# Attention, Fourier mixing and feed-forward on one core: radix-4 sums of four tiles as matrix products, and every tile's sums turned by TensorE

## The chip, the cores and the metric

The kernel runs on one core of a Trainium2 chip. The metric is the device time of one execution in microseconds (us). A core has a matrix engine (TensorE, PE in the rows, with its weight loads as PEld), a vector engine (VectorE, DVE), a scalar engine (ScalarE, ACT), GpSimd (POOL), and a queue engine (SyncE, SP), which here issues all DMA transfers but the gathers. Each engine works through its own list of instructions strictly in order; an instruction that waits holds everything behind it on its engine.

## What is computed

Inputs are q, k, v of shape 8 x 8 x 576 x 64 (batch, heads, positions, width of a head) and two weight matrices of 512 x 2048 and 2048 x 512, stored in double precision. The output has 8 x 576 rows of 512.

```
scores = scale * np.matmul(q, k.transpose(0, 1, 3, 2))
mask = (rel >= 0) & (rel < window)            # window = 64
attn = softmax(where(mask, scores, -1e9)); x = attn @ v   # heads side by side: 512 columns
mixed = np.real(fft(fft(x, axis=1), axis=2))
u = x + mixed
un = (u - mu) / np.sqrt(var + 1e-06)
ch = np.maximum(un @ w_ch1, 0.0) @ w_ch2
return u + ch
```

## The kernel before

**Tiles.** The 4608 rows are cut into 36 tiles of 128 rows (T = 0 to 35), nine tiles for each pair of batches. `attn_tile(T)` does the attention of a tile: keys and queries are transposed (pk, pq), scores of two half tiles are formed (psc), masked and reduced by DVE (L587), put through exp on ACT (L595), transposed (pp, pt), and multiplied with the values into two banks pa, one for each half of the heads (L657). DVE divides each by the row sums (rc, L665 to L669) into xu. Tiles 0 to 12 work in single precision and are transposed by TensorE ("whole"). From tile 13 on operands are split in two half-precision parts, high and low, laid side by side in SBUF, and transposed by DMA transposes that SP issues (kst L487, qbd L499, pt L626).

**The radix-4 results.** The Fourier transform along the 512 columns starts with sums and differences of the four column quarters of xu: `radix4` writes them to y (L691, four instructions on DVE, or on POOL). They must be turned so that columns lie on partitions. Where `soon` is true (tiles 0 to 12, and tiles 4 and 8 of each nine, by `Y_SOON`) TensorE transposes y into a PSUM bank py, one of the four banks that also hold scores and pa (L750), and ACT copies it into yT. Otherwise (17 tiles, from 14 to 34) y is split: ACT writes the high part yp (L754), DVE the low part (L758), SP issues one DMA transpose of both (L765), and POOL or DVE adds the turned parts into yT (L718). yp shares a ring of one buffer, "up", with the split normalised rows up (L1032, L1035).

**Then** `fft(b)` folds yT, does the two transform stages on TensorE (pg L878, pz L910), and SP stores the result md to memory (L938), for the first batch also straight to the rows' tile mt (L955). `norm_tile(T)` gathers mt, adds it to xu, normalises (L1005 to L1016), splits (u_hi, u_lo L1035) and turns the rows (L1040). `ffn(c)` takes two tiles at a time: 18 chunks of 16 steps, ph (L1197), relu and its low part hh by ACT and DVE (L1212, L1215), po (L1178). Chunk 0 works in single precision. The weights are 32 pieces of 512 KB, converted by three DVE instructions each (L1089 to L1101) and squared by ACT (L1107).

**What sets the order.** Steps are recorded with `op(engine, duration, priority, ...)`, some with a second engine (`alt`), and `Plan.order()` simulates the core with these durations and latencies and writes every engine's list from that. So a changed constant can move instructions everywhere. Where the plan foresees a longer gap of TensorE ahead of the first ph, it puts matmuls on the identity there that compute nothing (warm, L1276).

Of the kernel before, what the change touches and what calls it, by code (L numbers as in the profile page):

```python
# [12 lines left out]
F32 = mybir.dt.float32  # L13
# [6 lines left out]
ALU = mybir.AluOpType  # L20
# [21 lines left out]
Y_SOON = (4, 8)  # L42
LAZY, LAZY_FFT, LAZY_U = 0.4, 0.4, 0.5
# [5 lines left out]
SLACK = 0.5  # L49
PLAIN = 1  # L50
W_DMA, W_DMA_STEP, W_CONV, W_SQ, W_SPLIT, W_STEP = -40, 1.0, 20, 60, 60, 0.3
# [74 lines left out]
class Op:  # L126
    __slots__ = ("eng", "dur", "lat", "fn", "deps", "outs", "prio", "wait", "ready", "allocs", "bufs", "idx", "durs", "margin", "port", "slack")


class Plan:  # L130
# [13 lines left out]
    def __init__(self, rings, fifo):  # L144
        self.rings, self.fifo, self.ops, self.gaps = dict(rings), fifo, [], []
        self.slack = 0.0

    def op(self, eng, dur, prio, fn, reads=(), writes=(), lat=0.0, alt=(), holds=(), port=True):
# [5 lines left out]
        o.port, o.slack = port, self.slack  # L154
# [41 lines left out]
    def order(self):  # L196
# [23 lines left out]
        while len(res) < n:  # L220
# [77 lines left out]
def attn_fft_ffn_kernel(ctx: ExitStack, tc: tile.TileContext, q, k, v, w1, w2, gidx, dft_d, dft_s, mask, out):  # L298
# [24 lines left out]
    ident = cp.tile([P, P], F32, name="ident")  # L323
    mhalf = cp.tile([P, 1], F32, name="mhalf")
# [37 lines left out]
    op("POOL", 0.3, -500, lambda: make_identity(nc, ident), writes=[Bid])  # L362
    op("POOL", 0.1, -499, lambda: nc.gpsimd.memset(mhalf, -0.5), writes=[Bmh])
# [47 lines left out]
    def attn_tile(T, base):  # L411
# [18 lines left out]
        op("DMA", 1.45, base - 8, lambda: load("kn", "kq", k), writes=[bk], lat=2.0)  # L430
        op("DMA", 1.45, base - 8, lambda: load("qn", "kq", q), writes=[bq], lat=2.0)
        if whole:
            op("DMA", 1.45, base - 6, lambda: load("vw", None, v), writes=[Bva[i]], lat=2.0)
        else:
            op("DMA", 1.45, base - 6, lambda: load("vn", None, v), writes=[bv], lat=2.0)
# [39 lines left out]
        else:  # L475
# [27 lines left out]
            op("DMA", TURN, base + 0.2, k_turn, [bkp], [bkT], lat=2.0)  # L503
            op("ACT", 0.95, base + 0.5, lambda e: q_part(0, e), [bq], Bfl[4:6], alt=("DVE", 0.6, lazy))
            op("POOL", 2.1, base + 0.6, lambda e: q_part(1, e), [bq], Bfl[4:6], alt=("DVE", 1.13, lazy))
            for j in range(2):
                op("DMA", TURN, base + 0.7, lambda j=j: q_turn(j), Bfl[4:6], [Bq[i]], lat=2.8)
        if T == PRO and n > 0:
# [14 lines left out]
            op("DVE", 1.6, base + 0.3, k_tail, [BkT[(T - 1) % 3]], [BkT[before], Buf("tail")])  # L523
# [33 lines left out]
        for jj in range(2):  # L557
# [74 lines left out]
            op("DMA", HTURN, base + 4.2 + jj, lambda g=p_turn: g(0), [bpp], [bt, bt2], lat=1.8)  # L632
            op("DMA", HTURN, base + 4.3 + jj, lambda g=p_turn: g(1), [bpp], [bt2], lat=1.8)
# [5 lines left out]
        for hf in range(2):  # L639
# [668 lines left out]
```

## Time and profile before

| | |
|---|---|
| median of the runs | 1010.4 us |
| runs | 1010.17, 1010.4, 1551.11 us |
| the profiled execution's own time | 1014.19 us |
| its span, first to last instruction | 1012.4 us |
| mean granted TensorE clock | 0.990 of full speed |
| instructions | 22555 |

Read it so: the span is what the trace covers; 1.8 us of the profiled time lie outside it. Busy shares tell how full an engine is, not whether it is waited for. A busy TensorE is not TensorE at its peak, since its matmuls are pipelined and overlap in the records; what counts is the distance from one group's start to the next one's. A granted clock below 1.00 in a stretch means that part of it ran at 1.2 instead of 2.4 GHz. Many single-precision matmuls stand as two records each, so an x8 of psc is four matmuls.

### The profile page before, as it was taken

The numbers are of one execution on the slowest core, as the hardware profiler recorded it, in microseconds if no ns is written. First come the engines' busy times: TensorE is split into PE (matmuls) and PEld (weight loads), VectorE is DVE, ScalarE is ACT, GpSimd is POOL, SyncE is SP. The second block draws the span as 40 slices with busy tenths as digits, with TensorE's granted clock in tenths as the row PEclk, the third lists the DMA queues.
The fourth block names the chain that finished last, engine by engine and source line by source line (L and its number), as shares of the span: only waits on it lengthen the run. The fifth ranks groups of instructions, "written<-read, shape, count | busy, mean of one in ns | idle before, by whom it ended". The sixth has DMA issues, their size and how long they took to land.

```text
span 1012.4 us, 22555 instructions
## 1 busy us (share of the span) xinstructions
PE 975.3 (96%) x8793; PEld 692.1 (68%) x8793; DVE 671.6 (66%) x1972; ACT 417.3 (41%) x1044; POOL 205.8 (20%) x211
## 2 busy tenths in 40 slices
PE   8888999999998999999999999999999999999998
PEld 6776768766675666666676667666676667666664
DVE  5889898887876758676776668666786555441121
ACT  6665667563544444344452345322454223211111
POOL 1001001133224403352132203141121300310000
PEclk9988999999999999999999999999999999999999
DMA  8978766533859896988768575857564411220000
GB/s 192 232 199 232 188 193 146 103 72 75 148 124 167 168 152 137 163 151 148 152 127 169 101 137 106 160 117 149 90 128 103 83 32 45 63 63 21 1 21 22
DMA packets 310955, 123.60 MB, mean 122 GB/s; under 512 B 292728, under 2 KB 292856, under 8 KB 310848
## 3 DMA queue, kind: packets, MB, share of 16 engines
q1 hardware_dynamic: 308128, 113.24, 55.3%
q0 software_dynamic: 2720, 8.92, 3.2%
q8 instruction: 69, 1.13, 0.5%
q14 instruction: 38, 0.31, 0.1%
HBM read 54.97 MB, written 14.17 MB: 68 GB/s over the span
## 4 chain that ended last, share of the span: by engine, by line
PE 73%; DMA 10%; DVE 9%; SPq 3%; ACT 2%; issue 2%; POOL 1%; DVEq 0%; ACTq 0%; POOLq 0%
PE ph L1197 31%; PE po L1178 28%; PE pa L657 3%; PE pg L878 2%; PE pz L910 2%; PE psc L568 2%; DMA uhl<-up 2%; DMA pt<-flex 2%; PE psc L575 2%; DMA kn<-in_k 1%; DMA mt<-md,gix 1%; DVE hh L1215 1%; SPq L626 1%; DMA qn<-in_q 1%; DVE y L691 1%
## 5 line engine op out<-in xcount | busy, mean ns | idle before, releaser
L1197 PE MATMUL ph<-uhl,w0s 128*128 128x256 f16 (+1 forms) x3384 | 427.5, 277 | 9.3 <-DVE hh L1215 8.6
L1178 PE MATMUL po<-w1s,hh 128*128 128x512 f16 (+1 forms) x1696 | 426.0, 387 | 0.2
L1197 PEld LDWEIGHTS <-w0s 128*128 128x128 f16 x3264 | 318.5, 98 | 96.8 <-issue 14.3
L1215 DVE SCALAR_TENSOR_TENSOR hh<-ph,hh 128x256 f16<-128x256 f32 x272 | 114.6, 422 | 223.8 <-ACT hh L1212 212.2
L1212 ACT ACTIVATE hh<-ph 128x256 f16<-128x256 f32 x272 | 104.1, 383 | 375.5 <-PE ph L1197 264.5
L1178 PEld LDWEIGHTS <-hh 128*128 128x128 f16 x1632 | 155.9, 98 | 139.5 <-issue 1.0
L595 ACT ACTIVATE pr<-pr,nm 128x128 f32<-128x128 f32 x288 | 91.3, 393 | 16.3 <-DVE nm L587 16.3
L587 DVE CUSTOM_DVE_ANT_0 pr<-psc,mskb 128x128 f32<-128x128 f32 x288 | 65.7, 286 | 15.9 <-PE psc L568 11.8
L1012 POOL TENSOR_TENSOR rs<-mv,mhalf 128x1 f32<-128x1 f32 x36 | 21.6, 599 | 181.0 <-DVE mv L1008 160.2
L1035 POOL TENSOR_TENSOR up<-un,up 128x512 f16<-128x512 f32 x33 | 39.0, 1183 | 70.4 <-ACT up L403 63.6
L620 POOL TENSOR_TENSOR flex<-pr,flex 128x512 f16<-128x512 f32 x25 | 30.0, 1202 | 109.5 <-ACT flex L403 90.7
L657 PE MATMUL pa<-va,pt 128*64 128x65 f16 (+1 forms) x760 | 41.5, 207 | 5.7 <-DMA pt<-flex 5.1
L988 POOL DMA_INDIRECT mt<-md,gix x34 | 35.9, 1057 | 52.0 <-DMA md<-mp 46.4
L657 PE MATMUL pa<-ve,pt 128*64 128x65 f16 (+1 forms) x760 | 42.0, 208 | 0.1
L484 POOL TENSOR_TENSOR flex<-kn,flex 128x512 f16<-128x512 f32 x19 | 22.7, 1197 | 83.6 <-ACT flex L403 82.1
L403 ACT CAST flex<-pr 128x512 f16<-128x512 f32 x38 | 23.5, 620 | 27.7 <-DMA pt<-flex 25.5
L669 DVE TENSOR_TENSOR xu<-pa,rc 128x256 f32<-128x256 f32 x72 | 30.6, 425 | 2.9 <-DMA out<-xu 0.3
L568 PE MATMUL psc<-kst,qbd 128*128 128x128 f32 x208 | 29.8, 293 | 2.5 <-ACT qbd L403 1.2
L691 DVE TENSOR_TENSOR y<-xu 128x256 f32<-128x256 f32 x70 | 30.2, 472 | 0.6
L657 PEld LDWEIGHTS <-pt 128*64 128x64 f16 x1104 | 20.8, 112 | 14.0 <-issue 7.2
L568 PEld LDWEIGHTS psc<-kst,qbd 128*128 128x128 f32 x208 | 26.9, 203 | 4.5 <-issue 1.9
L910 PE MATMUL pz<-g,ds__75 97*96 97x257 f16 (+3 forms) x240 | 29.2, 273 | 0.5 <-DVE g L888 0.5
(156 smaller groups left out, 1115.1 us busy)
## 6 DMA issues: line engine op xcount, KB each, us to landing
wd<-in_moe_w_ch SPq DMA_DIRECT2D x20, 512.0 KB
out<-xu SPq DMA_DIRECT2D x36, 256.0 KB
ve<-va SPq DMA_DIRECT2D x67, 130.0 KB
kn<-in_k SPq DMA_DIRECT2D x32, 256.0 KB
qn<-in_q SPq DMA_DIRECT2D x32, 256.0 KB
flex<-in_moe_w_ch SPq DMA_DIRECT2D x12, 512.0 KB
flex<-in_v SPq DMA_DIRECT2D x20, 256.0 KB
md<-mp SPq DMA_DIRECT2D x24, 192.0 KB
```

Of the source, the lines that this page charges most:

```text
L568: nc.tensor.matmul(p_[:, hp], qw, keys(hp, jj), start=True, stop=True)
L587: nc.vector.tensor_tensor_reduce(out=t["pr", jj][:, hp], in0=t["ps", jj][:, hp], in1=mskb[:, m : m + P], scale=-0.125, scalar=3.0e38, op0= ...
L595: nc.scalar.activation(pr, pr, AF.Exp, bias=t["nm", jj][:, hp : hp + 1], scale=-1.0)
L657: nc.tensor.matmul(pa[64 * jj : 64 * jj + 64, hh], pt[:, sl], v_, start=(x == 0), stop=(x == len(mm) - 1))
L691: eng.tensor_tensor(out=o, in0=p0, in1=p1, op=al)
L910: nc.tensor.matmul(pz[:M, c0:c1], ds_[:NJ, a, c[0] : c[0] + c[1]], t["g", gi][:, b_, c0:c1], start=(x == 0), stop=(x == len(mm) - 1),)
L988: nc.gpsimd.indirect_dma_start(out=mts[T], out_offset=None, in_=mds[pb][0 : HR if n < 4 else 2 * HR], in_offset=bass.IndirectOffsetOnAxis( ...
L1035: eng.tensor_tensor(out=t["up"][:, 1], in0=t["un"], in1=t["up"][:, 0], op=ALU.subtract)
L1178: nc.tensor.matmul(t["po"][i], l_, r_, start=(f == 0 and x == 0), stop=(f == NKF - 1 and x == len(mm) - 1))
L1197: nc.tensor.matmul(ph, l_, r_, start=(x == 0), stop=(x == len(mm) - 1))
L1212: nc.scalar.activation(t["hh", f][:, 0], ph, AF.Relu)
L1215: nc.vector.scalar_tensor_tensor(out=hh[:, 1], in0=ph, scalar=0.0, in1=hh[:, 0], op0=ALU.max, op1=ALU.subtract)
```

## The change

Every tile now has `soon` true, so the two-part way (yp, its DMA transpose, the addition) is run no more. For tiles 1 to 4 `radix4` is not recorded at all: TensorE forms the sums itself while it turns the tile, as products of a quarter of xu with the identity or with its negative, added up in PSUM, 12 products in place of 4 transposes. The division by the row sums is cut in two, the reciprocal on DVE and the multiplication on DVE or ACT; on ACT it is four instructions of 64 columns, one for each head. Constants of the plan change: estimated DMA latencies rise, priorities of the weights' conversion fall, and a new margin makes steps on other engines start later behind their producers.

```diff
-Y_SOON = (4, 8)
-LAZY, LAZY_FFT, LAZY_U = 0.4, 0.4, 0.5
+Y_SOON = (0, 1, 2, 3, 4, 5, 6, 7, 8)
+LAZY, LAZY_FFT, LAZY_U = 0.4, 0.8, 0.2
-SLACK = 0.5
+SLACK = 1.0
+SLACK_V = 0.3
+WARY = 0
+LAZY_N = -0.8
+Y_SUMS = (1, 2, 3, 4)
-W_DMA, W_DMA_STEP, W_CONV, W_SQ, W_SPLIT, W_STEP = -40, 1.0, 20, 60, 60, 0.3
+W_DMA, W_DMA_STEP, W_CONV, W_SQ, W_SPLIT, W_STEP = -40, 1.0, 40, 70, 50, 0.3
...
+    op("POOL", 0.4, -480, lambda: nc.gpsimd.tensor_scalar(out=minus, in0=ident, scalar1=-1.0, scalar2=None, op0=ALU.mult), [Bid], [Bid])
...
-        op("DMA", 1.45, base - 8, lambda: load("kn", "kq", k), writes=[bk], lat=2.0)
+        op("DMA", 1.45, base - 8, lambda: load("kn", "kq", k), writes=[bk], lat=2.5)
...
+            def normed(eng, hf=hf):
+                pa, rc = t["pa", hf], t["rc", hf]
+                xv = xts[T].rearrange("p (h d) -> p h d", h=H)[:, 4 * hf : 4 * hf + 4]
+                if eng is nc.scalar:
+                    for hh in range(4):
+                        nc.scalar.mul(xv[:, hh], pa[:, hh, 0:64], rc[:, hh])
+                else:
+                    eng.tensor_tensor(out=xv, in0=pa[:, :, 0:64], in1=rc.to_broadcast([P, 4, 64]), op=ALU.mult)
...
-            op("DVE", 0.75, base + 6.2 + 0.5 * hf, normed, [bpa], [bx], port=False)
+            brc = Buf()
+            op("DVE", 0.26, base + 6.2 + 0.5 * hf, recip, [bpa], [brc], port=False)
+            op("DVE", 0.32, base + 6.25 + 0.5 * hf, normed, [bpa, brc], [bx], alt=("ACT", 0.95, LAZY_N), port=False)
...
-        op("POOL", 2.35, base + 7, radix4, [bx], [by], alt=("DVE", 1.2, LAZY_Y if T < 4 else lazy))
+        summed = T in Y_SUMS
+        if not summed:
+            op("POOL", 3.2, base + 7, radix4, [bx], [by], alt=("DVE", 1.2, LAZY_Y if T < 4 else lazy))
...
-            for j in range(4):
-                nc.tensor.transpose(t["py"][:, j], t["y"][:, j], ident)
+            for j, terms in enumerate(((0, 1, 2, 3), (0, 5, 2, 7), (0, 6), (1, 7))):
+                if summed:
+
+                    for x, m in enumerate(terms):
+                        quarter = xts[T][:, P * (m % 4) : P * (m % 4) + P]
+                        nc.tensor.matmul(
+                            t["py"][:, j], quarter, ident if m < 4 else minus, start=(x == 0), stop=(x == len(terms) - 1)
+                        )
+                else:
+                    nc.tensor.transpose(t["py"][:, j], t["y"][:, j], ident)
```

Three places show how the lists move. The first is TensorE at the turning of tile 1's radix-4 results (py1; pq3 and pk4 are later tiles' queries and keys, pp2 and psc2 tile 2's exponentials and scores). Before:

```order
L464 MATMUL pq3_392<-ident_69,qn3_318 128x128 x4
L606 MATMUL pp2_0_401<-ident_69,pr2_0_312 128x128 x4
L606 MATMUL pp2_1_414<-ident_69,pr2_1_348 128x128 x4
L464 MATMUL pk4_429<-ident_69,kn4_374 128x128 x4
...
L750 MATMUL py1_448<-ident_69,y1_420 128x128 x4
```

and now:

```order
L574 MATMUL psc2_0_382<-kst_80,qbd0_77 128x128 x4
L574 MATMUL psc2_1_393<-kst_80,qbd0_77 128x128 x4
L470 MATMUL pk3_407<-ident_69,kn3_313 128x128 x4
L769 MATMUL py1_422<-ident_69,xu1_353 128x128 x5
L769 MATMUL py1_422<-minus_70,xu1_353 128x128
...
L612 MATMUL pp2_0_450<-ident_69,pr2_0_381 128x128 x4
L612 MATMUL pp2_1_459<-ident_69,pr2_1_392 128x128 x4
```

Twelve products of xu1 stand where four transposes of y1 stood, and they stand ahead of tile 2's exponentials instead of behind them. The second place is TensorE around the first step of the feed-forward part (ph0; pu0 and pu1 are its turned rows of tiles 0 and 1). Before:

```order
L568 MATMUL psc7_0_1234<-kst_79,qbd1_77 128x128 x4
L464 MATMUL pk9_1246<-ident_69,kn9_1170 128x128 x4
L1028 MATMUL pu0_1259<-ident_69,un0_1251 128x128 x4
L606 MATMUL pp6_1_1269<-ident_69,pr6_1_1151 128x128 x4
L1028 MATMUL pu1_1276<-ident_69,un1_1257 128x128 x4
...
L568 MATMUL psc7_1_1312<-kst_79,qbd1_77 128x128 x4
L1197 MATMUL ph0_0_1324<-uhl0_1260,w0s_84 128x256 x4
```

and now:

```order
L1051 MATMUL pu0_1441<-ident_69,un0_1400 128x128 x4
L612 MATMUL pp8_0_1450<-ident_69,pr8_0_1268 128x128 x4
L1051 MATMUL pu1_1462<-ident_69,un1_1402 128x128 x4
L470 MATMUL pq9_1471<-ident_69,qn9_1367 128x128 x4
L612 MATMUL pp8_1_1478<-ident_69,pr8_1_1302 128x128 x4
L1220 MATMUL ph0_0_1491<-uhl0_1442,w0s_85 128x256 x4
```

The exponentials turned just ahead of the first ph are tile 8's instead of tile 6's: more of the attention stands ahead of the feed-forward part. The third place is SP's list in tiles 14 and 15 (md1 is a stored Fourier result, pt15 tile 15's exponentials, qbd0 its later neighbour's queries). Before:

```order
L938 DMA md1_3910<-mp2_1_3802 96x512
L765 DMA_TRANSPOSE py14_3917<-yp14_3842 128x8x128
L626 DMA_TRANSPOSE pt15_0_3934<-flex_78 128x8x64
L499 DMA_TRANSPOSE qbd0_76<-flex_78 128x16x64
L938 DMA md1_3910<-mp2_2_3823 96x512
...
L626 DMA_TRANSPOSE pt15_1_3986<-flex_78 128x8x64
L499 DMA_TRANSPOSE qbd0_76<-flex_78 128x16x64
L938 DMA md1_3910<-mp2_0_3948 96x512
```

and now:

```order
L505 DMA_TRANSPOSE qbd0_77<-flex_79 128x16x64
L632 DMA_TRANSPOSE pt15_0_3814<-flex_79 128x8x64
L632 DMA_TRANSPOSE pt15_1_3838<-flex_79 128x8x64
...
L433 DMA kn18_3969<-in_k 128x8x64
L433 DMA qn18_3993<-in_q 128x8x64
L961 DMA md1_4061<-mp2_1_3954 96x512
```

The transpose of yp14 is gone, and tile 15's turns stand ahead of the stores of md1 instead of between them.

## Rows read from the trace of the kernel before

**Rows 1.** The page's first part: busy time of each engine, share of the span, instructions.
```profile
span 1012.4 us, 22555 instructions
...
PE 975.3 (96%) x8793; PEld 692.1 (68%) x8793; DVE 671.6 (66%) x1972; ACT 417.3 (41%) x1044; POOL 205.8 (20%) x211
```
**Rows 2.** Busy time of each engine by stretch: the stretch, its length, busy time and instructions of PE, PEld, DVE, ACT and POOL, the granted clock, the DMA engines' busy share and GB/s.
```profile
0.00:93.00 93.00, 75.87 (x743) 64.36 (x744) 73.24 (x260) 57.57 (x149) 8.72 (x19) 0.91 0.86 215
93.00:300.00 207.00, 205.24 (x1681) 149.31 (x1681) 174.53 (x504) 116.58 (x287) 44.44 (x48) 1.00 0.60 134
300.00:800.00 500.00, 486.45 (x4850) 336.93 (x4849) 349.45 (x1035) 204.82 (x511) 135.60 (x126) 1.00 0.73 137
800.00:1013.00 213.00, 207.75 (x1524) 141.54 (x1522) 74.36 (x176) 38.34 (x99) 17.06 (x18) 1.00 0.14 35
...
0.00:67.00 67.00, 56.12 (x558) 47.73 (x559) 49.28 (x187) 42.74 (x108) 5.90 (x16) 0.92 0.91 216
```
**Rows 3.** TensorE in order of time between 66 and 103 us: start, length, group; in brackets the idle time before it and what ended it.
```profile
69.22 5.62 PE L1276 MATMUL warm<-ident 128*128 128x256 f16 x50
78.55 1.36 PE L606 MATMUL pp<-ident,pr 128*128 128x128 f32 x4 [3.70 <-ACT pr L595]
...
87.40 1.16 PE L568 MATMUL psc<-kst,qbd 128*128 128x128 f32 x8 [0.68 <-ACT pt L403]
88.40 0.60 PE L464 MATMUL pk<-ident,kn 128*128 128x128 f32 x4
...
93.05 5.34 PE L1197 MATMUL ph<-uhl,w0s 128*128 128x256 f32 x24
...
102.69 0.60 PE L750 MATMUL py<-ident,y 128*128 128x128 f32 x4
103.13 1.45 PE L1178 MATMUL po<-w1s,hh 128*128 128x512 f32 x3
```
**Rows 4.** The chain that ended last, pieces of its first 93 us: start, length, what.
```profile
14.24 1.08 PE pa L657 x32
...
40.77 4.99 DMA va<-in_v
...
48.71 6.80 DMA qn<-in_q
```
**Rows 5.** DMA issues by line: how many, KB of each.
```profile
wd<-in_moe_w_ch SPq DMA_DIRECT2D x20, 512.0 KB
...
ve<-va SPq DMA_DIRECT2D x67, 130.0 KB
kn<-in_k SPq DMA_DIRECT2D x32, 256.0 KB
```
**Rows 6.** Who TensorE waited for over the whole span: us in total, times, longest.
```profile
PE ph L1197 <- DVE hh L1215: 8.6, 13, 1.7
PE pa L657 <- DMA pt<-flex: 5.1, 4, 3.2
```
**Rows 7.** SP in order of time from 293 to 305 us.
```profile
293.25 1.25 SPq L765 DMA_TRANSPOSE py<-yp  x1
294.59 1.23 SPq L626 DMA_TRANSPOSE pt<-flex  x1
...
303.94 1.19 SPq L626 DMA_TRANSPOSE pt<-flex  x1
```
**Rows 8.** The DMA transposes of yp (line 765): durations min/median/max in ns on SP's sequencer, first and last start.
```profile
L765 SPq DMA_TRANSPOSE py<-yp x17: 1232/1247/2175, 293.3 to 811.1; - x17
```
**Rows 9.** SP's own waits ahead of these transposes: us in total, times, longest.
```profile
SPq L765 <- DVE yp L758: 20.4, 5, 7.2
...
SPq L765 <- DVE g L888: 12.8, 3, 7.5
```
**Rows 10.** Busy time by stretch, columns as in rows 2, for ten microseconds behind the longest wait of rows 6.
```profile
310.00:320.00 10.00, 10.00 (x64) 6.74 (x63) 7.06 (x25) 4.49 (x11) 3.47 (x5) 0.87 0.93 168
```
**Rows 11.** TensorE in order of time there, its first feed-forward groups behind that wait.
```profile
309.76 2.74 PE L1197 MATMUL ph<-uhl,w0s 128*128 128x256 f16 x12
312.29 1.59 PE L1178 MATMUL po<-w1s,hh 128*128 128x512 f16 x6
```
**Rows 12.** Groups of instructions by line: line, engine, operation, out<-in, shapes, count | busy us, mean ns of one | idle time of the engine just before them, and what ended it.
```profile
L595 ACT ACTIVATE pr<-pr,nm 128x128 f32<-128x128 f32 x288 | 91.3, 393 | 16.3 <-DVE nm L587 16.3
...
L1035 POOL TENSOR_TENSOR up<-un,up 128x512 f16<-128x512 f32 x33 | 39.0, 1183 | 70.4 <-ACT up L403 63.6 <-DVE up L407 3.8 <-issue 3.0
...
L669 DVE TENSOR_TENSOR xu<-pa,rc 128x256 f32<-128x256 f32 x72 | 30.6, 425 | 2.9 <-DMA out<-xu 0.3
...
L1276 PE MATMUL warm<-ident 128*128 128x256 f16 x129 | 19.4, 305 | 1.4 <-POOL ident masks.py:199 1.4
...
L758 DVE SCALAR_TENSOR_TENSOR yp<-y,yp 128x512 f16<-128x512 f32 x17 | 13.3, 783 | 3.0 <-ACT yp L403 2.9
...
L403 ACT ACTIVATE yT<-py 128x512 f32<-128x512 f32 (+2 forms) x21 | 10.7, 518 | 12.2 <-PE py L750 11.9
...
L403 ACT ACTIVATE yp<-y 128x512 f16<-128x512 f32 x16 | 10.1, 630 | 18.7 <-DVE y L691 11.3 <-DMA uhl<-up 7.4
...
L718 DVE TENSOR_TENSOR yT<-py 128x512 f32<-128x512 f16 x9 | 6.2, 691 | 7.4 <-DMA py<-yp 7.4
...
L927 ACT COPY mp<-pz 96x2 f32<-96x2 f32 (+1 forms) x24 | 4.1, 173 | 0.0
...
L1035 DVE TENSOR_TENSOR up<-un,up 128x512 f16<-128x512 f32 x1 | 0.7, 691 | 0.0
```

More of the change, by code (lines that the diff above doesn't have):

```diff
@@ L126 @@
 class Op:
-    __slots__ = ("eng", "dur", "lat", "fn", "deps", "outs", "prio", "wait", "ready", "allocs", "bufs", "idx", "durs", "margin", "port", "slack")
+    __slots__ = ("eng", "dur", "lat", "fn", "deps", "outs", "prio", "wait", "ready", "allocs", "bufs", "idx", "durs", "margin", "port", "slack", "wary")
 class Plan:
@@ L323, in attn_fft_ffn_kernel @@
     ident = cp.tile([P, P], F32, name="ident")
+    minus = cp.tile([P, P], F32, name="minus")
     mhalf = cp.tile([P, 1], F32, name="mhalf")
@@ L506, in attn_tile @@
             for j in range(2):
-                op("DMA", TURN, base + 0.7, lambda j=j: q_turn(j), Bfl[4:6], [Bq[i]], lat=2.8)
+                op("DMA", TURN, base + 0.7, lambda j=j: q_turn(j), Bfl[4:6], [Bq[i]], lat=3.0)
         if T == PRO and n > 0:
@@ L521, in k_tail @@
                     nc.vector.tensor_tensor(out=lo, in0=old, in1=hi, op=ALU.subtract)
-            op("DVE", 1.6, base + 0.3, k_tail, [BkT[(T - 1) % 3]], [BkT[before], Buf("tail")])
+            op("DVE", 3.0, base + 0.3, k_tail, [BkT[(T - 1) % 3]], [BkT[before], Buf("tail")])
         def v_part(z):
@@ L767, in attn_tile @@
         if soon:
-            op("PE", 0.44, base + 8, flip_y, [by, Bid], [bpy, *first])
+            op("PE", 2.85 if summed else 0.44, base + 8, flip_y, [bx if summed else by, Bid], [bpy, *first])
         else:
@@ L772, in attn_tile @@
             op("DVE", 0.6, base + 7.6, y_lo, [by], [byp])
-            op("DMA", TURN, base + 7.7, y_turn, [byp], [bpy], lat=2.2)
+            op("DMA", TURN, base + 7.7, y_turn, [byp], [bpy], lat=3.0)
         for a in keeps:
@@ L942, in fft @@
             op("PE", 0.67 if cl == 0 else 1.32, base + 5, sstage, [*(bg[gi] for _, gi in use), Bds], [bpz, bmp])
-            op("ACT", 0.65, base + 5.1, odd, [bpz], [bmp])
-            op("DVE", 1.2, base + 5.2, mix, [bpz], [bmp], port=False)
+            op("ACT", 0.39, base + 5.1, odd, [bpz], [bmp])
+            op("DVE", 1.03, base + 5.2, mix, [bpz], [bmp], port=False)
             if b == 0:
@@ L1115, in weight_piece @@
         op("DVE", 0.6, pr - 0.2, lambda: conv(2), bw, [bf])
-        op("ACT", 0.72, W_SQ + W_STEP * order, square, [bf], [bj, Bssq[x]])
+        op("ACT", 0.53, W_SQ + W_STEP * order, square, [bf], [bj, Bssq[x]])
     def weight_scale(x, prio):
```

29 lines of the change are left out of this document (13 added, 16 removed).

## The prediction

> **What bounds the kernel now.** I read the busy times first. TensorE is busy for 975.3 of 1012.4 us, DVE for 671.6, ACT for 417.3 [rows 1]. The reader is to see that TensorE is the bound, but an average can hide a stage with another limit, so the stretches come next. After 93 us TensorE is busy for 899.4 of 919.4 us; nearly all the rest is 13.6 us between 300 and 800 us and some 5 at the end [rows 2]. Before 93 us it is busy for 75.9 us, at a mean granted clock of 0.91, so part of that ran at 1.2 GHz [rows 2]. And of those 75.9 us, 19.4 are warm matmuls, which compute nothing and all stand ahead of the first ph [rows 12]. So the kernel has two stages. In the prologue, to the first ph at 93.05 us [rows 3], TensorE has 17.1 us idle and 19.4 us of filler, 36.5 us that other work could use; DVE is busy for 73.2 us and the DMA engines for 0.86 of it [rows 2], and the chain of waits runs through loads that take 5.0 and 6.8 us [rows 4]. After it, time is TensorE work plus its few waits.
>
> Who TensorE waits for there is in the waits: 8.6 us in 13 waits for hh, and 5.1 us in four waits for turned exponentials pt, the longest 3.2 us [rows 6]. That one can be followed on SP's list: the transpose of yp takes 1.25 us ahead of three sets of pt transposes, the last of which is issued at 303.94 us [rows 7].
>
> **The change part by part.** All sums are made against the profiled execution: span 1012.4 us [rows 1] plus 1.8 us outside it, 1014.2 us. It is 3.8 us above the median of the runs, 1010.4 us; I take differences from it and apply them to the median.
>
> *Turning on TensorE.* Four transposes take 0.44 us, from one group's start to the next one's (102.69 to 103.13 us) [rows 3]. 17 tiles gain them. But what counts is what stands behind the first ph. In the lists 20 transposes of y stand ahead of it before and 12 after, out of 76 and 128, so behind it stand 56 and 116: 60 more, at 0.11 us each +6.6 us.
>
> *Work moved ahead.* The new list has more attention ahead of the first ph: four more transposes of queries and 16 of exponentials (0.44 us for four, 2.2 us), eight more score products (four take 1.00 us, 87.40 to 88.40 us [rows 3]; 2.0 us), and one tile's products with the values (1.08 us [rows 4]). That is 5.3 us less behind it. TensorE's work behind the first ph thus changes by 6.6 - 5.3 = +1.3 us.
>
> *Start of the first ph.* What the prologue takes in is 4 x (3.0 - 0.44) = 10.2 us for the products of tiles 1 to 4 (12 products, priced as the score products of the same shape, 1.00 us for four) and the 5.3 us above, 15.5 us, against 36.5 us free; the warm matmuls fall from 129 to 91, which by 5.62 us for 50 [rows 3] is 4.3 us. So TensorE has room. DVE has the same work: by the lists it loses two tiles' radix-4 sums and all 12 multiplications ahead of that point, and gains two tiles' masks. What grows is loading. Ahead of the first store of the Fourier result (mt) SP's list has 12 weight pieces instead of 10, 27 loads of q, k and v instead of 25, and 15 copies of values instead of 13: 2 x (512 + 256 + 130) KB [rows 5], 1.84 MB, at the 216 GB/s of the first 67 us 8.5 us. The DMA engines' free share there, 9% of 67 us, is 6.0 us [rows 2]. I take the part that does not fit, +2.5 us. The bounds are +8.5 us, if all of it lies on the chain, and -5.0 us, if the later placed copies of values no longer hold SP for the 5.0 us that the chain shows [rows 4].
>
> *The y transposes and SP.* 17 transposes at 1.25 us leave SP's list, and with them 33.2 us in which SP stood waiting for yp with everything queued behind it [rows 8, 9]. What that is worth is bounded by TensorE's waits for transposes: 5.1 us, and the slow clock behind the longest: the granted clock of the ten us after it is 0.87, TensorE having stood idle for 3.2 us before, and 12 ph matmuls take 2.53 us there to the next group (309.76 to 312.29) [rows 10, 11]; 13% of ten us is 1.3 us. So 0 to -6.4 us. Since tile 15's turns now stand ahead of the md stores and no y transpose is among them, I take most of it, -5.0 us.
>
> *DVE and ACT around hh.* 58 of 72 multiplications go from DVE to ACT, 42 of them behind the first ph. DVE behind it sheds 42 x 0.425 = 17.9 us, 13.3 us of yp and 6.2 us of additions, and takes over 25 of POOL's up instructions at 0.69 us, +17.3 us [rows 12]: about -20 of 598 us. ACT gets four instructions of 64 columns for each; none of this size is in the trace. Between the 2-column copy (173 ns) and the 128-column exponential (393 ns) [rows 12] four take 0.7 to 1.6 us; I take 1.0, nearer the larger form by width, so +42 us, plus 17 copies of py at 0.52, minus 10.1 us of yp [rows 12]: some +41 on 360 us. ACT stays under half busy, but an hh can queue behind a block of four. Today's 72 pairs of exponential blocks (four instructions, over 1 us) coexist with 8.6 us of waiting for hh [rows 6]; if they were its whole cause, one costs 0.12 us and 42 more cost +5 us. If the relief on DVE ends the waits, it is -8.6 us. Here I take -3.0 us, the side of DVE, on which these waits end.
>
> *PSUM.* py of 17 tiles now takes one of the four banks of scores and pa until ACT has copied it. No wait of TensorE for such a copy is in the trace; I cost it at nothing, since feed-forward matmuls in other banks cover it, and at 17 x 0.52 = 8.8 us without that cover [rows 12].
>
> The sum is +1.3 + 2.5 - 5.0 - 3.0 = -4.2 us: 1010.0 us for a profiled execution, 1006.2 us beside the median. I give 1006.
>
> **The rivals.** First, *the products lengthen the prologue.* For it: each set holds TensorE for 3.0 us and stands ahead of the next tile's exponentials, on a core that runs partly at 1.2 GHz there [rows 2]. Against it: 36.5 us are free. If all 10.2 us come through in place of the 2.5, the time is 1010.4 + 1.3 + 10.2 - 8.0 = 1013.9 us, slower than before; it decides from the point where the first ph starts later than 93.05 + 6.7 = 99.8 us. The Trainium skill speaks for this rival: Perfetto Trace Analysis, Optimizing Tensor Performance, Transposes, asks for the transpose operation wherever a matrix is only turned, since it skips the arithmetic that a standard matmul does. By that rule turning by products is the dearer way, and the rows of this trace agree (1.00 against 0.44 us for four); whether it shows in the time is what the free 36.5 us decide.
>
> Second, *ACT becomes the engine that is waited for.* For it: 42 more blocks of four, and ACT feeds every hh. Against it: ACT is busy for 205 of 500 us in the middle [rows 2]. With +5 us for hh in place of -3.0 the time is 1010.4 + 1.3 + 2.5 - 5.0 + 5.0 = 1014.2 us, and 1019 if pt waits remain as well.
>
> Third, *nearly every wait goes:* -5.0 at the start, -6.4, -8.6 and +1.3 us give 991.7 us. For it: the lists put producers earlier everywhere. Against it: a new order has waits of its own.
>
> **How the numbers follow.** The forecast has 0.58, from 998 to 1011 us by itself. The products' rival has 0.16, ACT's 0.14, the third 0.12. To leave out no more than 2 in 10 the range reaches from 995 to 1018 us. A measurement tells about 2% from no change here, which is 20 us: below 990 us lies only what is beyond the third rival, part of the prologue's 36.5 us given back, 0.05; above 1031 us would need the full 8.8 us of PSUM or the full loads on top of a rival, 0.04; within it 0.91.
>
> **What would show it.** The first ph between 91 and 100 us shows the prologue's step; earlier than 88 or later than 100 refutes it. In TensorE's waits, those for pt should fall below 2 us and those for hh to some 5.6. The four-instruction block on ACT should take about 1.0 us. The group py should take 0.44 us a tile by transposes, and 3.0 by products. SP should have no waits for yp. The forecast is wrong if TensorE's idle time behind the first ph grows, or if its clock is low in a new place.

## The result, and the profile after

The changed kernel takes 1021.39 us (median of 9 runs, 1015.31 to 1023.33), the kernel before 1012.43 us beside it; the ratio is 1.0082 with a 95% interval of 1.0064 to 1.01. It is slower by about 8.3 us (the ratio is of means, and leaves out the one run of 1551.11 us of the kernel before), outside the range of 995 to 1018 us and on the other side of no change from the 1006 us that were forecast. The profiled execution took 1019.44 us against 1014.19 us: the two traces hold 5.2 us of the loss, since the one of before lies above its median and the one of after below.

The page of the kernel after, first part, as in [rows 1]:

```profile
span 1017.7 us, 22903 instructions
...
PE 986.9 (97%) x8903; PEld 705.6 (69%) x8903; DVE 654.3 (64%) x1908; ACT 461.9 (45%) x1275; POOL 168.5 (17%) x169
```

TensorE gained 11.6 us of busy time and DVE lost 17.3 us. Where the time went, the windows tell (columns as in [rows 2]: length, busy time of PE, PEld, DVE, ACT, POOL, clock, DMA share, GB/s):

```profile
0.00:67.00 67.00, 59.90 (x603) 53.20 (x603) 42.85 (x179) 49.35 (x147) 6.22 (x17) 0.95 0.98 216
0.00:99.80 99.80, 85.60 (x861) 76.23 (x862) 72.68 (x283) 75.06 (x227) 8.55 (x20) 0.94 0.94 220
40.00:52.00 12.00, 9.35 (x61) 8.69 (x61) 7.54 (x29) 6.60 (x22) 0.20 (x1) 0.72 1.03 233
99.80:1017.00 917.20, 901.26 (x8044) 629.34 (x8042) 581.59 (x1626) 386.88 (x1049) 159.93 (x149) 1.00 0.53 106
```

TensorE in order of time, in two pieces (start, length, group; in brackets the idle time before it and what ended it):

```profile
43.73 1.12 PE L470 MATMUL pk<-ident,kn 128*128 128x128 f32 x4 [2.65 <-ACT xu L680]
44.64 2.46 PE L769 MATMUL py<-ident,xu 128*128 128x128 f32 x10
...
49.87 1.08 PE L612 MATMUL pp<-ident,pr 128*128 128x128 f32 x8
...
95.55 1.08 PE L1051 MATMUL pu<-ident,un 128*128 128x128 f32 x4 [4.03 <-ACT pr L601]
...
99.84 2.55 PE L1220 MATMUL ph<-uhl,w0s 128*128 128x256 f32 x8
```

The first ph starts at 99.84 us, 6.8 us later than the 93.05 us of [rows 3]. Behind it TensorE's busy time is 901.3 us against 899.4 us in [rows 2], and from the first ph to TensorE's last matmul it is 913.7 us against 915.3 us. So the whole loss of the two traces lies in the prologue; what was to come back behind it, 6.7 us, was 1.6 us. The granted clock ahead of the first ph is 0.94 here and was 0.91 before, so over the whole prologue the clock is not what was lost.

The chain that ended last, pieces from 30 to 70 us (start, length, what), to be held against [rows 4]:

```profile
30.01 1.15 PE pa L663 x30
...
34.87 7.05 DMA flex<-in_moe_w_ch
...
41.94 0.43 DVE w1s L1112
...
42.75 0.94 ACT xu L680 x4
...
43.73 1.12 PE pk L470 x4
44.84 5.23 PE py L769 x24
...
51.50 1.38 PE pa L663 x32
...
55.30 2.69 PE py L769 x24
...
63.01 6.65 DMA kn<-in_k
```

The reader is to follow one wait. A weight piece takes 7.05 us to land. DVE stands in front of its conversion (w1s), with tile 3's reciprocal behind it in DVE's list; ACT's multiplication waits for that, TensorE for ACT. TensorE idles for 2.65 us, and its clock, 1.00 in the window 0 to 40 us, is 0.72 in the 12 us that follow, so part of them ran at 1.2 GHz: tile 3's twelve products take 5.23 us there, tile 4's 2.69 us later. Tile 4's products with the values start at 51.5 us instead of the 43.7 us of before:

```profile
43.67 0.27 PE L657 MATMUL pa<-ve,pt 128*64 128x65 f32 x1
```

A delay of some 7 us stays to the first ph; whether this wait is its cause is tried in e3. DVE's waits for weights ahead of the first ph, after (us in total, times, longest):

```profile
DVE w1s L1112 <- DMA flex<-in_moe_w_ch: 5.2, 2, 3.6
DVE w0s L1112 <- DMA wd<-in_moe_w_ch: 3.0, 2, 2.4
```

and before, where it waited for weights 1.0 us:

```profile
DVE w0s L1089 <- DMA flex<-in_moe_w_ch: 1.0, 1, 1.0
```

TensorE's waits behind the first ph, to be held against [rows 6]:

```profile
PE ph L1220 <- DVE hh L1238: 9.2, 11, 2.8
PE py L773 <- DVE y L704: 2.3, 3, 1.6
```

Those for pt are gone, those for hh are not less, and those for y were 0.9 us before. Groups by line, as in [rows 12]:

```profile
L680 ACT ACTIVATE xu<-pa,rc 128x64 f32<-128x64 f32 x232 | 52.2, 323 | 22.6 <-DVE rc L673 9.8 <-DVE rc L670 9.2 <-PE pa L663 3.5
...
L1300 PE MATMUL warm<-ident 128*128 128x256 f16 x91 | 14.1, 301 | 1.3 <-POOL ident masks.py:199 1.3
```

### The profile page after: what moved, and what is told of

Its sections match the earlier page's. It is cut to its first block, busy times and chain, and to the rows that moved or that the text cites. A ratio compares the mean times of both kernels' runs of the same rounds, so it can differ in the third digit from the quotient of the medians.

```text
span 1017.7 us, 22903 instructions
## 1 busy us (share of the span) xinstructions
PE 986.9 (97%) x8903; PEld 705.6 (69%) x8903; DVE 654.3 (64%) x1908; ACT 461.9 (45%) x1275; POOL 168.5 (17%) x169
## 4 chain that ended last, share of the span: by engine, by line
PE 80%; DVE 7%; DMA 6%; SPq 3%; ACT 2%; issue 1%; DVEq 0%; ACTq 0%
PE ph L1220 34%; PE po L1201 32%; PE pa L663 3%; PE pz L933 2%; PE pg L901 2%; PE psc L581 2%; DMA qbd<-flex 2%; DMA kn<-in_k 1%; PE psc L574 1%; PE py L773 1%; DVE hh L1238 1%; PE py L769 1%; DVE y L704 1%; DMA wd<-in_moe_w_ch 1%; SPq L505 1%
## 5 line engine op out<-in xcount | busy, mean ns | idle before, releaser
L1220 PE MATMUL ph<-uhl,w0s 128*128 128x256 f16 (+1 forms) x3384 | 427.9, 277 | 10.1 <-DVE hh L1238 9.2
L680 ACT ACTIVATE xu<-pa,rc 128x64 f32<-128x64 f32 x232 | 52.2, 323 | 22.6 <-DVE rc L673 9.8
L626 POOL TENSOR_TENSOR flex<-pr,flex 128x512 f16<-128x512 f32 x29 | 37.2, 1289 | 100.8 <-ACT flex L409 89.0
L501 POOL TENSOR_TENSOR flex<-qn,flex 128x1024 f16<-128x1024 f32 x16 | 34.9, 2180 | 71.2 <-ACT flex L409 38.4
L490 POOL TENSOR_TENSOR flex<-kn,flex 128x512 f16<-128x512 f32 x14 | 19.1, 1366 | 87.3 <-ACT flex L409 71.1
L1039 DVE TENSOR_SCALAR un<-xu,mv,rs 128x512 f32<-128x512 f32 x36 | 30.3, 844 | 0.8 <-POOL rs L1035 0.7
L409 ACT CAST flex<-pr 128x512 f16<-128x512 f32 x44 | 26.9, 614 | 7.0 <-DMA pt<-flex 5.3
L409 ACT ACTIVATE yT<-py 128x512 f32<-128x512 f32 (+2 forms) x39 | 20.6, 539 | 20.8 <-PE py L773 17.1
L704 DVE TENSOR_TENSOR y<-xu 128x256 f32<-128x256 f32 x64 | 27.8, 475 | 1.7 <-ACT xu L680 1.6
L574 PE MATMUL psc<-kst,qbd 128*128 128x128 f32 x208 | 26.8, 280 | 1.6 <-ACT qbd L409 1.6
```

Source lines behind the costliest of these rows:

```text
L409: nc.scalar.mul(out, in_, scale) if scale is not None else nc.scalar.copy(out, in_)
L626: eng.tensor_tensor(out=pp[:, :, 1], in0=t["pr", jj], in1=pp[:, :, 0], op=ALU.subtract)
L680: nc.scalar.mul(xv[:, hh], pa[:, hh, 0:64], rc[:, hh])
L704: eng.tensor_tensor(out=o, in0=p0, in1=p1, op=al)
L1220: nc.tensor.matmul(ph, l_, r_, start=(x == 0), stop=(x == len(mm) - 1))
```

## The experiments

Three theories stood at the start. *Loads:* the transfers ahead of the Fourier part hold the prologue. *Products:* the twelve products of tiles 1 to 4 lengthen TensorE's part of it. *ACT:* the four-instruction division on ACT holds what waits for it. Medians are of 4 to 11 runs, ratios against the kernel before on the same chip, with the 95% interval.

The first ph is read from one trace of each run, and it scatters. The last run of the next part, e17, leaves everything ahead of the first ph as it is in the changed kernel, and its trace has

```profile
98.15 2.34 PE L1221 MATMUL ph<-uhl,w0s 128*128 128x256 f32 x8
```

That is 1.7 us earlier than 99.84 us, with the same instructions in the same order. So a difference of less than about 2 us between two first phs shows nothing by itself.

### One part at a time, every list held as in the changed kernel

**e1_one_term:** one product for each quarter, 4 in place of 12.

```diff
             for j, terms in enumerate(((0, 1, 2, 3), (0, 5, 2, 7), (0, 6), (1, 7))):
                 if summed:
+                    terms = terms[:1]
```

> The changed kernel with the same lists, but each of the four turned quarters of tiles 1 to 4 is one product instead of two to four: 4 products a tile in place of 12 (the radix-4 sums are left out there). 'Products' theory: the groups of 12 hold TensorE ahead of the next exponentials, so with 4 of them, 1.0 instead of 2.8 us each, the first ph starts 6 to 8 us earlier than 99.8 us, at 92 to 94 us, and the time falls by as much. 'Loads' theory: the chain waits for weight pieces and keys that land late, so the first ph moves by 0 to 2 us only, to 98 to 100 us. 'Division on ACT' theory: 0 to 2 us.

1017.3 us, 1.004 [1.002, 1.0061]. The windows 0 to 67 and 40 to 52 us, and the first ph:

```profile
0.00:67.00 67.00, 53.67 (x547) 43.53 (x547) 45.32 (x191) 51.42 (x155) 6.23 (x17) 1.00 1.02 226
40.00:52.00 12.00, 8.26 (x82) 6.64 (x81) 9.55 (x35) 8.36 (x29) 1.71 (x1) 1.00 1.09 241
```

```profile
97.04 0.81 PE L1221 MATMUL ph<-uhl,w0s 128*128 128x256 f32 x3
```

The clock is whole, and the first ph comes 2.8 us earlier than in the changed kernel's own trace, 1.1 us earlier than in e17's; 4 us are left over before. The ratio falls from 1.0082 to 1.004, 4.2 us, by intervals that do not meet. Products are a part, not all.

**e2_one_division:** the division on ACT with one instruction in place of four.

```diff
-                    for hh in range(4):
-                        nc.scalar.mul(xv[:, hh], pa[:, hh, 0:64], rc[:, hh])
+                    nc.scalar.mul(xv, pa[:, :, 0:64], rc[:, 0])
```

> The changed kernel with the same lists, but where ACT does the division by the row sums it is one instruction of 256 columns instead of four of 64 (all four heads get the first head's factor). 'Division on ACT' theory: the pairs of blocks take 0.9 instead of 1.75 us and stand on the chain of all five first tiles, so the first ph starts 4 us or more earlier, at 96 us or before, and hh waits fall from 9.2 us to under 6. 'Loads' and 'products' theories: the first ph moves by less than 2 us.

1017.77 us, 1.0044 [1.0024, 1.0064]; first ph at 99.1 us. TensorE's wait for hh does not fall:

```profile
PE ph L1219 <- DVE hh L1237: 9.3, 10, 3.0
```

So ACT's blocks of four are not what hh waits for, and the 0.7 us at the first ph are less than its scatter. Yet the ratio falls by 0.0038, 3.8 us, nearly as much as in e1, though the two intervals touch at 1.0064. ACT's blocks may be a part of the loss as well; where those 3.8 us lie is not shown.

**e3_conv_no_wait:** the conversions of the weights read a small constant tile and wait for no load; all loads stay.

```diff
-            lo, hi = w["raw"][:, :, 0], w["raw"][:, :, 1]
+            raw = still[:, None, :].to_broadcast([P, 512, 2])
+            lo, hi = raw[:, :, 0], raw[:, :, 1]
```

> The changed kernel with the same lists and the same transfers, but the weights' conversions read a small constant tile instead of the loaded pieces, so DVE waits for no weight load (the weights are left out). 'Loads' theory, in its form that DVE stands in its list behind conversions of pieces that land late: the 3.6 us wait near 38 us and the later ones go, TensorE's clock does not fall near 44 us, and the first ph starts 4 to 7 us earlier, at 93 to 96 us. If only the volume of the loads matters, by the keys and values that come late, 0 to 2 us. 'Products' theory: 0 to 2 us.

1019.08 us, 1.0062 [1.004, 1.0083]; first ph at 98.8 us. The wait of the chain above is gone, and TensorE waits for keys instead, 5.1 us against 1.8 us in the changed kernel:

```profile
PE pk L471 <- DMA kn<-in_k: 5.1, 2, 2.7
```

With that wait gone the first ph comes 1.0 us earlier, less than its scatter, and the ratio's interval overlaps that of the changed kernel. So DVE's place behind this wait is not the cause by itself: without it, the next load is waited for.

**e4_quarter_weights:** weight loads of 128 KB in place of 512 KB.

```diff
-            nc.sync.dma_start(w["raw"].rearrange("p c z -> p (c z)"), src)
+            nc.sync.dma_start(w["raw"].rearrange("p c z -> p (c z)")[:, 0:256], src[:, 0:256])
...
-            lo, hi = w["raw"][:, :, 0], w["raw"][:, :, 1]
+            raw = w["raw"][:, 0:1].to_broadcast([P, 512, 2])
+            lo, hi = raw[:, :, 0], raw[:, :, 1]
```

> The changed kernel with the same lists, but each weight piece's load moves a quarter of its columns, 128 instead of 512 KB (the weights are left out; conversions wait for the load and read its first pair). 'Loads' theory: both the conversions and the keys come earlier, the first ph starts 6 us or more earlier, at 93.5 us or before, and the DMA engines' share ahead of it falls from above 0.9 to 0.7 or less. 'Products' theory: the first ph moves by less than 2 us.

1012.4 us, 0.9996 [0.9972, 1.002]: the whole loss is back. The window, the first ph, and the chain:

```profile
40.00:52.00 12.00, 11.97 (x126) 11.34 (x124) 11.47 (x49) 11.52 (x40) 1.71 (x1) 1.00 0.81 181
```

```profile
92.46 0.81 PE L1221 MATMUL ph<-uhl,w0s 128*128 128x256 f32 x3
```

```profile
30.12 1.15 PE pa L663 x30
...
33.69 2.68 PE py L769 x24
...
37.78 1.38 PE pa L663 x32
...
41.65 2.94 PE py L769 x24
...
46.02 1.38 PE pa L663 x32
```

From tile 2's pa to tile 4's it is 15.9 us here, in two steps of about 8, against 21.5 us in the changed kernel. The chain is now TensorE's own, with the products on it.

**e9_before_quarter_weights**, the control: the same edit in the kernel before.

> The kernel before with weight loads of 128 KB in place of 512 KB, lists unchanged; it leaves out three quarters of each weight piece. It is the control for the same cut in the changed kernel, which brought its first ph from 99.8 to 92.5 us. If the 1.84 MB of loads that the change adds ahead of the first store of mt are the cause, the prologue of before was not loaded to that point, and its first ph moves by 3 us or less, to 90 us or later, the time to 1009 us or above. If loads hold both prologues alike, it moves by 6 us or more, to 87 us or earlier, and the time to about 1005 us: then the added TensorE work in front is the cause and the loads only a common burden.

1005.81 us, 0.9942 [0.9919, 0.9965].

```profile
87.47 0.81 PE L1198 MATMUL ph<-uhl,w0s 128*128 128x256 f32 x3
```

This takes most of e4 away from the loads theory: less loading moves the first ph of before by 5.6 us too. Loads hold both prologues, and what is special to the change is 7.4 - 5.6 = 1.8 us of it, about the scatter of a first ph. In the times it is 0.0086 - 0.0058 = 0.0028, 2.8 us, which intervals of this width do not tell from nothing. With small loads in both, the changed kernel's first ph is still 5.0 us later.

**e10_quarter_one_term:** e1 and e4 together.

> The changed kernel with both cuts: weight loads of 128 KB, and one product per quarter in place of two to four (it leaves out three quarters of each weight piece and 8 of the 12 products of tiles 1 to 4). One product alone gave 2.8 us at the first ph, the small loads alone 7.3 us. If the two causes add up, the first ph is at 89 to 90 us. If TensorE carries the chain once the loads are gone, the whole 7 us of products shows: first ph at 85 to 87 us, time about 1005 us. If something third holds the prologue, it stays at 91 to 92.5 us.

1012.43 us, 1.0004 [0.9986, 1.0023].

```profile
90.76 0.81 PE L1222 MATMUL ph<-uhl,w0s 128*128 128x256 f32 x3
```

With small loads the products are worth 92.5 - 90.8 = 1.7 us at the first ph, as much as it scatters, and nothing in the time (1.0004 against e4's 0.9996). 3.3 us at the first ph against e9 belong to neither cut, and in the time it is more: 1.0004 against 0.9942 is 6.3 us, by intervals far apart. The rest of that lies behind the first ph, 915.4 us to the last matmul against e9's 912.6.

**e17_transposes_twice:** the transposes of y of tiles 13 to 35 done twice.

```diff
-                    nc.tensor.transpose(t["py"][:, j], t["y"][:, j], ident)
+                    for again in range(1 if T < 13 else 2):
+                        nc.tensor.transpose(t["py"][:, j], t["y"][:, j], ident)
```

> The changed kernel with the transposes of y of tiles 13 to 35 done twice, lists unchanged otherwise: 23 x 4 more transposes at 0.11 us, 10.1 us more work on TensorE behind the first ph. If TensorE's work there comes through in full, the time is about 1031 us (1021 plus 10). If half of it disappears in waits that are there anyhow (12.5 us of idle time), it is 1025 to 1027 us. The first ph stays within 1 us of 99.8 us.

1023.53 us, 1.0127 [1.01, 1.0153]. The group of transposes (92 more than the changed kernel's 128) and the window behind the first ph, which starts at 98.1 us:

```profile
L774 PE MATMUL py<-ident,y 128*128 128x128 f32 x220 | 29.6, 274 | 3.8 <-DVE y L704 3.8
```

```profile
98.10:1020.00 921.90, 910.41 (x8136) 639.26 (x8134) 578.72 (x1628) 386.60 (x1049) 158.76 (x149) 1.00 0.51 106
```

TensorE is busy for 9.2 us more (10.1 were worked out), but from the first ph to the last matmul it is 918.5 us against 913.7, 4.8 us more, and the ratio rises by 0.0045, 4.6 us (the two intervals just touch at 1.01). About half of the added work is paid out of waits: those for hh are 5.5 us here, 9.2 us in the changed kernel.

### Parts put together anew, lists written again by the plan

Here a part is taken out or put in and `Plan.order()` writes all lists again.

**e5_y_only:** the kernel before, `Y_SOON = (0, 1, 2, 3, 4, 5, 6, 7, 8)`.

> The kernel before with one change: every tile's radix-4 results are turned by TensorE, nothing else (no products, division as before, constants as before). SP's list has the same 13.21 MB of loads ahead of the first store of mt as before. Loads theory: the first ph starts within 1.5 us of before's 93.1 us, and the time differs from before's only by what happens behind it: 17 turns at 0.44 us (+7.5 us) less the waits for pt (up to -6.4 us), so 1012 to 1015 us. Rival, the turning itself costs the time (PSUM banks held by py, +8.8 us uncovered): about 1020 us, all of it behind the first ph.

1017.71 us, 1.0046 [1.0028, 1.0063]; first ph at 92.9 us, from there 919.2 us to the last matmul (915.3 before). TensorE's waits for pt:

```profile
PE pa L657 <- DMA pt<-flex: 1.8, 3, 0.8
```

Turning alone leaves the prologue as it was, takes most of the waits for pt away, and still costs some 5 us: 68 transposes more, 7.5 us, are not paid by the waits.

**e6_no_products:** the changed kernel, `Y_SUMS = ()`.

> The changed kernel with its constants, its division cut in two and all tiles turned by TensorE, but with no products: tiles 1 to 4 go through radix-4 sums and transposes again. The loads ahead of the first store of mt stay at 15.0 MB. Loads theory: the first ph starts at 96 to 98 us, as in the run with one product per quarter, and the time is 1016 to 1018 us. Products theory: with the 10 us of products gone the first ph starts at 93 us or earlier and the time is 1010 to 1013 us.

1011.42 us, 0.9992 [0.997, 1.0014]; first ph:

```profile
97.05 0.69 PE L1220 MATMUL ph<-uhl,w0s 128*128 128x256 f32 x2
```

The fastest version here that leaves nothing out, not told apart from before and 9 us faster than the changed kernel by the ratios. At the first ph it gains the same 2.8 us as e1; behind it it is 5.1 us shorter (908.6 us), with lists of its own, and its waits for hh are 5.0 us in place of 9.2.

**e18_two_tiles:** the changed kernel, `Y_SUMS = (1, 2)`.

> The changed kernel with products for tiles 1 and 2 only; tiles 3 and 4 go through radix-4 sums and transposes. If the 10 us between products for four tiles (1021.4 us) and for none (1011.4 us) follow their number, this is 1015 to 1018 us, with the first ph at 98 to 99 us. If only the products of tiles 3 and 4 hurt, which stand where TensorE runs at the low clock, it is 1011 to 1013 us with the first ph near 97 us. If the difference is a matter of the lists and not of the products, it can fall anywhere between 1008 and 1025 us and the first ph does not follow the number.

1019.72 us, 1.0081 [1.0058, 1.0104]; first ph at 98.1 us. With 4, 2 and 0 tiles by products the first ph starts at 99.8, 98.1 and 97.0 us. That looks like 0.7 us for a tile, but e17 starts at 98.1 us with four tiles, so a dose is not shown. What follows the first ph does not go by their number: 913.7, 915.7 and 908.6 us.

**e8_no_products_dve:** the changed kernel, `Y_SUMS = ()` and `LAZY_N = 1e9`, so that DVE does the whole division. **e15_products_dve:** only `LAZY_N = 1e9`.

> The changed kernel with its constants, but with no products and with the whole division on DVE. By the plan the loads ahead of the first store of mt go back to 13.2 MB. Loads theory: the first ph starts at 92 to 94 us, and the time is 1009 to 1013 us. If the changed constants alone are the cause (weights' conversion later in the lists, longer estimated latencies), the first ph stays at 97 us or later and the time at 1017 us.

> The changed kernel with products, turning and constants, but the whole division on DVE. If the division on ACT is the cause of the slowdown (ACT waited for), this is faster than the changed kernel: 1014 us or less. If it is a gain, as between the two versions without products, this is slower by some 10 us: about 1030 us. If products cost nothing once DVE does the division, it equals the version with neither, 1021.7 us.

e8: 1021.67 us, 1.0085 [1.0053, 1.0116], first ph at 94.8 us, 920.9 us behind it. e15: 1024.0 us, 1.0114 [1.0081, 1.0147], 99.4 and 923.1 us. The division on ACT is no loss beside the new constants: by the ratios it is worth 9 us without products (e8 to e6) and 3 us with them (e15 to the changed kernel; the intervals overlap). The products cost 2 us here, not 10, by intervals that overlap too, though the first ph comes 4.6 us later with them.

**e13_no_products_no_turning:** the changed kernel, `Y_SUMS = ()`, `Y_SOON = (4, 8)`. **e16_division_and_turning:** the changed kernel, `Y_SUMS = ()`, with the constants of before. **e14_division_only:** e16 with `Y_SOON = (4, 8)`.

```diff
-LAZY, LAZY_FFT, LAZY_U = 0.4, 0.8, 0.2
+LAZY, LAZY_FFT, LAZY_U = 0.4, 0.4, 0.5
...
-SLACK = 1.0
-SLACK_V = 0.3
+SLACK = 0.5
+SLACK_V = 0.0
...
-W_DMA, W_DMA_STEP, W_CONV, W_SQ, W_SPLIT, W_STEP = -40, 1.0, 40, 70, 50, 0.3
+W_DMA, W_DMA_STEP, W_CONV, W_SQ, W_SPLIT, W_STEP = -40, 1.0, 20, 60, 60, 0.3
...
-        op("DMA", 1.45, base - 8, lambda: load("kn", "kq", k), writes=[bk], lat=2.5)
+        op("DMA", 1.45, base - 8, lambda: load("kn", "kq", k), writes=[bk], lat=2.0)
```

> The changed kernel with its constants and its division on ACT, but without products and with the two-part way for 17 tiles as before. If turning by itself costs the 5 us that it cost the kernel before (1017.7 against 1012.4 us), this is 1011.4 less 5: 1005 to 1008 us. If the two-part way's waits for turned exponentials come back and weigh as much as the turns, it stays at 1010 to 1013 us. The first ph stays near 97 us, with 15.0 MB of loads ahead.

> The kernel before with one part of the change: the division in two, its multiplications on DVE or ACT; no products, two-part way and constants as before. The attention groups ahead of the first ph are those of before. If the division on ACT is a gain by itself (10 us between the two versions without products), the time is 1002 to 1007 us, nearly all of it behind the first ph. If that gain was the lists' and not the division's, the time is 1010 to 1015 us. If moved attention is the rest of the prologue's loss, the first ph starts at 93 to 94 us here.

> The kernel before with two parts of the change: the division in two with multiplications on ACT, and every tile turned by TensorE; no products, constants as before. The attention groups ahead of the first ph are those of before. If the parts add up it is the division alone plus 5 us. If turning costs nothing once DVE is relieved, it is within 1 us of the division alone. The first ph starts at 93 to 94 us if neither part touches the prologue.

e13: 1014.54 us, 1.0027 [1.0007, 1.0046]. e14: 1027.5 us, 1.0155 [1.0117, 1.0193]. e16: 1024.85 us, 1.0118 [1.0086, 1.0151]. All three times went against what was expected of them. TensorE's longest waits in e14:

```profile
PE ph L1220 <- DVE hh L1238: 10.5, 11, 1.9
PE ph L1220 <- DMA uhl<-up: 8.5, 2, 7.8
```

The parts do not add. The division on ACT costs 15 us beside the old constants without turning and gains 9 us beside the new ones. Turning costs 5 us in the kernel before; in each pair with the division on ACT (e14 to e16, e13 to e6) the time falls by some 3 us instead, a size at which the intervals still overlap.

**e7_weights_later:** the changed kernel with a weight load's latency in the plan at 6.0 in place of 2.5. **e12_two_weights_later:** the changed kernel with `W_DMA` 20 in place of -40. **e11_no_products_weights_later:** the same with `Y_SUMS = ()`.

> The changed kernel with one number altered: the plan's estimated latency of a weight load, 6.0 instead of 2.5 us, which puts 7 weight pieces ahead of the first store of mt instead of 12 (12.4 MB instead of 15.0 MB); products, division and turning stay. Loads theory: 2.6 MB at 216 GB/s is 12 us of transfers fewer ahead of the store, so the first ph starts at 92 to 95 us although eight more score products and a tile's products with the values stand ahead of it (3 us), and the time is 1010 to 1013 us. Products theory: the first ph stays at 98 to 100 us and the time at 1018 us or above.

> The changed kernel with its products and with the weight loads' priority 20 instead of -40: 10 weight pieces ahead of the first store of mt instead of 12 (13.7 MB instead of 15.0 MB); one tile's products with the values more stand ahead of the first ph (1.1 us). Loads theory: the first ph comes at 96 to 97.5 us instead of 99.8 and the time is 1016 to 1018 us. If TensorE's added work holds it, the first ph stays at 99 to 101 us and the time at 1020 us or above.

> The changed kernel without products (tiles 1 to 4 through radix-4 sums and transposes) and with the weight loads' priority 20 instead of -40, which puts 10 weight pieces ahead of the first store of mt instead of 12 (13.5 MB instead of 15.0 MB); TensorE's groups ahead of the first ph keep their number. Loads theory: the first ph comes at 93 to 95 us instead of 97.0, and the time is 1007 to 1010 us, below before's. If the chain of DVE's steps and not the loads holds this version, the first ph stays at 96 to 98 us and the time at 1011 us or above.

e7: 1080.02 us, 1.0664 [1.0628, 1.07], first ph at 98.9 us. e12: 1018.84 us, 1.0063 [1.005, 1.0077], 99.5 us. e11: 1030.39 us, 1.0182 [1.0167, 1.0197], 98.4 us. TensorE's longest waits in e7:

```profile
PE ph L1220 <- DVE w0s L1124: 27.8, 7, 9.9
PE po L1201 <- DVE w1s L1124: 12.7, 6, 3.3
```

Fewer weight pieces ahead of the stores do not bring the first ph forward, against the loads theory, and the weights are then missing behind it.

## Why the prediction was wrong

**The step that failed first** is the start of the first ph: +2.5 us was given, +6.8 us came (+5.1 us in e17's trace of the same prologue). That lies inside the bounds of -5.0 and +8.5 and inside the 91 to 100 us that were to show the step, so these were too wide to tell it from its rival. The term was priced by the loads alone; of that the runs show 1.8 us, by difference (e4 against e9) and not clear of the scatter. What failed is the sentence that TensorE has room: 15.5 us of added work were set against 36.5 us free, and laid on the prologue at nothing. TensorE's work ahead of the first ph, warm matmuls left out, grew by 15.0 us, from 75.9 - 19.4 to 85.6 - 14.1, much as was given. But of the 36.5 us only 8.2 were given back: the idle time fell from 17.1 us to 99.8 - 85.6 = 14.2, the warm matmuls from 19.4 to 14.1 us. The other 6.8 us are the delay. This is bookkeeping: it tells that the room was not used, not why. The chain gives a reason that no run isolates: the rest of the free time stands where TensorE waits for a load or for a chain of other engines, and an engine's work cannot be put there.

How the loss divides is known in part. The products are worth 4.2 us of the time with full loads and 1.1 to 2.8 us at the first ph (e1), but nothing in the time with small loads (e10 against e4). With both cut, 3.3 us at the first ph and 6.3 us of the time are left (e10 against e9) that no run assigns. The attention moved ahead (5.3 us) fits the first, but e14 and e16 keep the attention of before, have no products, and still start the first ph at 95.8 and 94.9 us. That stays open.

**The second step that failed** is hh: -3.0 us was taken, from 8.6 to 5.6, and it is 9.2. DVE behind the first ph did shed 598.3 - 581.6 = 16.8 us, near the 20 given, but hh does not wait for DVE's load as a whole, nor for ACT's blocks (e2). The trace shows what the longest of the 11 waits stands behind: instructions of DVE ahead of hh, above all one that took 2.37 us, where the median of its line and tile is 0.56, while POOL worked on another tile.

```profile
373.90 2.44 POOL L501 TENSOR_TENSOR flex<-qn,flex 128x1024 f16<-128x1024 f32 x1
374.39 2.37 DVE L845 SCALAR_TENSOR_TENSOR h<-h,yT 128x388 f32<-128x388 f32 x1
377.75 2.72 PE L1220 MATMUL ph<-uhl,w0s 128*128 128x256 f16 x12 [2.77 <-DVE hh L1238]
```

The second longest, 1.35 us at 446.36 us, stands behind another (L1039, 2.24 us for 0.54), again beside POOL's L501; the two are 4.1 of the 9.2 us. Behind the first ph of the changed kernel 27 instructions of DVE took more than twice the median of their line and tile and at least 0.7 us more, 32.7 us too much in sum, and in every one POOL was at work for half of the time or more, though it is busy for only 160 of the 917 us (its spans in a profile are rough). In the kernel before there are 20, with 20.8 us, and its longest waits for hh, 1.7 and 1.4 us, stand behind DVE's waits for loads. So the longest waits come from single late instructions, which a lighter DVE does not remove. That POOL causes it is read from the coincidence; no run took POOL's work away, and the other waits for hh have other places in the lists.

**What held.** Work on TensorE behind the first ph: +1.3 given, 901.26 - 899.44 = +1.8 measured. The waits for pt: gone, as the -5.0 said, and no wait of SP for yp is left. (Of the 33.2 us that the prediction put down to yp, [rows 9] put 12.8 down to g; no term of the sum uses them.) Prices: 2.69 us for twelve products (3.0 given), 0.94 us for ACT's block of four (1.0 given). PSUM at nothing: e5's 7.5 us of transposes cost 3.9 us behind the first ph, so py's bank adds nothing that can be seen.

**The signs.** TensorE's idle time behind the first ph did not grow: it was 919.4 - 899.4 = 20.0 us and is 917.2 - 901.3 = 15.9. A low clock in a new place did come, 0.72 in 40 to 52 us where before had 1.00, but before had its own low stretch, 0.86 in 28 to 40 us, and the mean ahead of the first ph rose.

**The rivals.** The first had its sign, and its signpost was met, a first ph at 99.84 us where 99.8 decided; but by luck of one execution, since the same prologue came at 98.15 us in e17. Its cause is only a part, 4.2 of the 8.3 us of time and not the whole prologue, and its time of 1013.9 us is far below what was measured. The Trainium skill (Perfetto Trace Analysis, Optimizing Tensor Performance, Transposes) wants a turn done by the transpose operation and not by a matmul; here 2.69 us against 0.44 us a tile, and leaving the products out gave the fastest version, so these runs agree. The second, ACT, failed in the way that it was told, by waits for hh (e2), and beside the new constants the division on ACT is no loss (e8, e15). As a cost elsewhere it is not ruled out: e2's 3.8 us, and e14's 15 us beside the old constants. Of the third only the waits for pt came true.

**The loss beyond the traces.** The two traces differ by 5.2 us, the medians by 9.0. Single executions of the changed kernel spread over 8 us, and the profiled ones are one of them each; the terms above are those of the traces, and what makes the rest is not shown.

## What to carry to other kernels

Idle time and filler in a stage that a chain bounds need not be room: here 8 of 36 us were given back; look first which gaps the new work's own inputs reach. When a cut cures the changed kernel, make the same cut in the old one before naming the cause; here three quarters of the cure at the first ph were common to both. Trace the same stretch twice before reading a difference of a microsecond or two in it; here it moved by 1.7 us on its own. Where a planner writes the lists, hold them fixed to price a part: written again, the same part was worth +15 or -9 us.

## What the runs showed that was not expected

Around one idle stretch of 2.65 us on TensorE the granted clock was 0.72 over 12 us, and the twelve products behind it took 5.23 us instead of 2.69. A product of single precision costs 2.69 / 12 = 0.22 us here, twice a transpose of the same shape (0.44 / 4). Of the 9.2 us of work that e17 put on a TensorE busy for 98% of its stage, about half reached the time. Instructions of DVE that took more than twice their usual time, and 0.7 us or more beyond it, had POOL at work beside them in all 27 cases behind the first ph. Weight loads, a background stream by their use, were worth 5.6 us of the kernel before.
